# Channel mixer over nine groups of 512 tokens in place of sixteen pieces of 320 and 256

## The chip, the cores and the metric

The kernel runs on one core of a Trainium2 chip. The metric is device time in microseconds (us), from the first to the last instruction, lower is better. TensorE (PE) multiplies, VectorE (DVE) and ScalarE (ACT) work on vectors, GpSimd (POOL) does elementwise work beside them, and the queue of SyncE (SP) issues all DMAs of this kernel. Each engine takes its instructions in a fixed order and waits on semaphores for the others.

## The reference

Eight batches of 576 tokens, eight heads of 64 channels. Heads 0 to 3 attend to a query's last 32 positions, heads 4 to 7 to earlier positions of the same residue modulo 32. The result, 512 channels a token, goes through a token mixer (576 to 256 to 576 positions) and a channel mixer (512 to 1536 to 512 channels), each with its residual:

```python
mask_local = (rel >= 0) & (rel < stride)
mask_strided = (rel >= 0) & (pos[None, :] % stride == pos[:, None] % stride)
...
attn_out = softmax(where(mask, q @ k.T / sqrt(64), -1e9)) @ v
x = attn_out.transpose(0, 2, 1, 3).reshape(B, S, H * D)
h = relu(x.transpose(0, 2, 1) @ w_tok1) @ w_tok2
u = x + h.transpose(0, 2, 1)
return u + relu(u @ w_ch1) @ w_ch2
```

The mixers' weights come as float64. The kernel cuts every operand of a mixer into a high and a low fp32r part and adds three products (high by high, high by low, low by high).

## The kernel before

**Local heads** (`local_unit`) are done in units of three chunks of 128 tokens and two heads, six units for a pair of batches: loads lq, lk, lv (L125 to L127), scores on PE (L133), softmax on DVE and ACT, transposes, products with v, and xl written to DRAM.

**Strided heads** are done in two ways. Those of batches 0 and 1 are on PE (`strided_pe`: scores L221, exponentials, transposes, products, then ex on DVE, L249, which goes to DRAM as xs, L259); their operands eq, ek, ev come by `strided_load`. Those of batches 2 to 7 are on GpSimd and VectorE (`strided`): after loads of sa and sb (L266, L267), 18 products of rising width, 64 to 1152 elements (L275, POOL), each followed by a reduce into ss (L276, DVE), a softmax, the load of v into sa, again 18 products (L290) and reduces into sb (L291), and four DMAs to xs. This text calls that work of one batch a pass, its halves the QK half and the AV half, and the passes of batches 2 to 7 in a row the lane. The tiles sa and sb have one buffer each, so a pass loads its operands after the one before has done with them.

**The token mixer** loads a batch's x (L299, L301), cuts it into xh (ACT, L313) and xlo (DVE, L314), multiplies by w_tok1 (`tok1`, L323, 56 matmuls of 256 columns a batch), cuts the hidden values into hh and hl, and in `tok2` transposes x (L341) and adds the products with w_tok2 (L346); the result is cut into uh (ACT, L349) and ul (DVE, L350).

**The channel mixer** (`mlp`) works on a piece, the 320 or the 256 tokens that one batch has in `PIECES`. For each of 12 chunks of the hidden size, `up_proj` does 12 matmuls into h (L439), cut into gh (ACT, L442) and gl (DVE, L443), and `down_proj` 12 matmuls into the four accumulators acc (L451): 288 matmuls a piece, 16 pieces. Midway, POOL adds uh and ul into ot (L464); at the end DVE adds acc to ot (L468) and DMAs bring the columns to out_t (L471 to L474).

**Order of the work.** The program is built as one long list, and a scheduler with a simulated timeline sets a fixed order on each engine from it. Other work is put into the list between the steps of a piece by the tables `ins0` and `ins1`: `tok2` of the same batch's second piece, late local units of the next pair, `do_load`, `do_tok1` and `do_tok2` of the next batch, and `do_strided(b + 2)`, which lists a pass two batches ahead at a lower priority. During piece 0 the last weights are loaded and cut (`do_pieces`; w_raw, L83) and batch 1's strided heads go between on PE; `second_ends` closes their pool and lists the first pass, batch 2's, at the second step of piece 1.

## Time and profile before

| what | value |
|---|---|
| median of 3 runs | 912.22 us (911.15 to 917.72) |
| span of the profiled execution | 912.1 us |
| mean granted TensorE clock in it | 0.979 |
| TensorE busy | 871.2 us, 96% of the span |
| VectorE busy | 514.4 us, 56% |
| GpSimd busy | 408.9 us, 45% |
| ScalarE busy | 261.5 us, 29% |

The profiled execution's span is 0.1 us from the median, so sums are made against 912.1. Rows of the profile give an engine, a line (L439 is line 439 of the kernel), an operation and the tiles as output<-inputs; xN is a count. In rows in order of time the first two numbers are the start and the length in us, and what stands in square brackets is idle time ahead of the instruction and what ended it. Matmuls are pipelined: a matmul's length is longer than the distance to the next one, and it is the distance that costs.

### The profile page before, as it was taken

The page shows a single profiled execution, that of the slowest core. Times are in us where ns is not written, and L with a number is a line of the kernel's source. Part 1 is how long each engine was busy: PE and PEld are TensorE (multiplying, and loading weights), DVE is VectorE, ACT ScalarE, POOL GpSimd, SP SyncE. Part 2 cuts the span into 40 slices and gives each one's busy share as a digit, 9 for nine tenths or more (in the row PEclk, how much of TensorE's full clock was granted, in tenths as well). Part 3 has the DMA queues.
Part 4 walks back from the last instruction along what each step waited for, and adds up shares of the span by engine and source line. Part 5 has one row for each costly group of instructions (what it writes and reads, how often), then busy time and mean ns, then how long its engine had stood idle before and what let it go on. Part 6 is the DMA issues. An engine that isn't in the chain of part 4 may idle for free.

```text
span 912.1 us, 20133 instructions
## 1 busy us (share of the span) xinstructions
PE 871.2 (96%) x8176; PEld 823.4 (90%) x8176; DVE 514.4 (56%) x1308; ACT 261.5 (29%) x840; POOL 408.9 (45%) x322
## 2 busy tenths in 40 slices
PE   6798999999989799999998999999999999999998
PEld 4667989899989599999998899898999999999998
DVE  2978794787478647757767864787232231222121
ACT  4755563222222123222231222322232221121111
POOL 0324342789397567959657594967001010101010
PEclk9968999999999699999999999999999999999999
DMA  8566644030642133230362024211131020100010
GB/s 249 174 212 192 198 152 132 28 95 23 175 137 80 55 105 89 75 105 24 95 175 57 27 81 129 88 53 50 47 108 32 1 81 1 30 1 24 1 31 24
DMA packets 71289, 78.36 MB, mean 86 GB/s; under 512 B 24100, under 2 KB 60068, under 8 KB 71196
## 3 DMA queue, kind: packets, MB, share of 16 engines
q1 hardware_dynamic: 71196, 77.07, 28.5%
q8 instruction: 64, 1.05, 0.5%
q14 instruction: 29, 0.24, 0.1%
HBM read 58.63 MB, written 18.28 MB: 84 GB/s over the span
## 4 chain that ended last, share of the span: by engine, by line
PE 64%; DVE 13%; DMA 9%; POOL 8%; SPq 2%; ACT 2%; issue 2%; DVEq 0%; POOLq 0%; ACTq 0%
PE h L439 24%; PE acc L451 23%; PE t L346 6%; POOL sprod L275 6%; PE t L323 5%; DVE xlo L314 5%; PE t L341 2%; POOL sprod L290 2%; DMA sb<-in_ks 2%; DVE ss L276 2%; DVE sb L291 1%; DMA x<-xs 1%; DVE w_f L89 1%; DVE w_f L88 1%; DMA w_raw<-in_wt 1%
## 5 line engine op out<-in xcount | busy, mean ns | idle before, releaser
L439 PE MATMUL h<-uh,w1h 128*128 128x320 f32 (+1 forms) x768 | 227.6, 300 | 3.9 <-DVE gl L443 3.2
L439 PE MATMUL h<-uh,w1l 128*128 128x320 f32 (+1 forms) x768 | 229.0, 299 | 0.0
L439 PE MATMUL h<-ul,w1h 128*128 128x320 f32 (+1 forms) x768 | 228.6, 299 | 0.0
L451 PE MATMUL acc<-gl,w2h 128*128 128x320 f32 (+1 forms) x768 | 227.3, 299 | 0.0
L451 PE MATMUL acc<-gh,w2l 128*128 128x320 f32 (+1 forms) x768 | 223.9, 299 | 0.0
L451 PE MATMUL acc<-gh,w2h 128*128 128x320 f32 (+1 forms) x768 | 220.1, 300 | 2.3 <-ACT gh L442 1.6
L275 POOL TENSOR_TENSOR sprod<-sb,sa 128x64 f32<-128x64 f32 (+8 forms) x108 | 160.2, 1517 | 63.0 <-DMA sb<-in_ks 47.6
L443 DVE SCALAR_TENSOR_TENSOR gl<-h,gh 128x320 fp32r<-128x320 f32 (+1 forms) x192 | 86.2, 452 | 163.4 <-ACT gh L442 163.2
L290 POOL TENSOR_TENSOR sprod<-sa,ss 128x64 f32<-128x64 f32 (+8 forms) x108 | 154.9, 1468 | 47.2 <-DVE ss L285 23.0
L464 POOL TENSOR_TENSOR ot<-uh,ul 128x320 f32<-128x320 f32 (+1 forms) x64 | 52.5, 836 | 262.5 <-DMA out_t<-ot 251.2
L442 ACT ACTIVATE gh<-h 128x320 fp32r<-128x320 f32 (+1 forms) x192 | 78.0, 409 | 309.9 <-PE h L439 309.4
L439 PEld LDWEIGHTS h<-uh,w1h 128*128 128x128 f32 x768 | 145.8, 191 | 5.6 <-DVE gl L443 4.0
L439 PEld LDWEIGHTS h<-uh,w1l 128*128 128x128 f32 x768 | 146.3, 191 | 0.6
L439 PEld LDWEIGHTS h<-ul,w1h 128*128 128x128 f32 x768 | 146.4, 191 | 0.3
L451 PEld LDWEIGHTS acc<-gl,w2h 128*128 128x128 f32 x768 | 146.0, 190 | 0.7 <-DVE gl L443 0.2
L451 PEld LDWEIGHTS acc<-gh,w2h 128*128 128x128 f32 x768 | 142.1, 190 | 4.5 <-ACT gh L442 1.8
L451 PEld LDWEIGHTS acc<-gh,w2l 128*128 128x128 f32 x768 | 144.8, 190 | 0.9
L276 DVE TENSOR_REDUCE ss<-sprod 128x1 f32<-128x64 f32 (+8 forms) x108 | 83.8, 780 | 43.1 <-POOL sprod L275 42.7
L291 DVE TENSOR_REDUCE sb<-sprod 128x64 f32<-128x64 f32 (+8 forms) x108 | 83.8, 780 | 26.6 <-POOL sprod L290 25.9
L314 DVE TENSOR_TENSOR xlo<-x,xh 128x256 fp32r<-128x256 f32 x80 | 66.9, 852 | 49.3 <-ACT xh L313 49.2
L323 PE MATMUL t<-xlo,t1h 128*128 128x256 f32 (+1 forms) x160 | 51.7, 333 | 13.5 <-DVE xlo L314 13.4
L313 ACT CAST xh<-x 128x256 fp32r<-128x256 f32 x80 | 32.1, 406 | 107.6 <-PE t L323 65.2
(79 smaller groups left out, 1080.7 us busy)
## 6 DMA issues: line engine op xcount, KB each, us to landing
w_raw<-in_w SPq DMA_DIRECT2D x24, 512.0 KB
out_t<-ot SPq DMA_DIRECT2D x64, 128.0 KB
lv<-in_vw SPq DMA_DIRECT2D x20, 384.0 KB
lk<-in_kT SPq DMA_DIRECT2D x20, 208.0 KB
x<-xs SPq DMA_DIRECT2D x8, 512.0 KB
lq<-in_qT SPq DMA_DIRECT2D x20, 192.0 KB
x<-xl SPq DMA_DIRECT2D x7, 512.0 KB
sa<-in_qs SPq DMA_DIRECT2D x6, 576.0 KB
```

What stands on the lines that cost most here:

```text
L275: nc.gpsimd.tensor_tensor(out=pr, in0=k_t[:, :n, :], in1=q_t[:, i:i + 1, :].to_broadcast([P, n, D]), op=ALU.mult)
L276: nc.vector.tensor_reduce(out=s_t[:, i, :n], in_=pr, axis=AX.X, op=ALU.add)
L290: nc.gpsimd.tensor_tensor(out=pr, in0=v_t[:, :, :n], in1=s_t[:, i:i + 1, :n].to_broadcast([P, D, n]), op=ALU.mult)
L291: nc.vector.tensor_reduce(out=o_t[:, i], in_=pr, axis=AX.X, op=ALU.add)
L314: nc.vector.tensor_tensor(out=xlo, in0=x, in1=xh.bitcast(F32), op=ALU.subtract)
L323: nc.tensor.matmul(ph[m][:, o:o + DT], l, r, start=(c == 0 and k == 0 and o == 0), stop=(short and k == 1 and o + DT == n), skip_group_che ...
L346: nc.tensor.matmul(pu[:, :n], l[:, cs], r[:, m, s0:s0 + n], start=False, stop=(m == 1 and k == 2), skip_group_check=True)
L439: nc.tensor.matmul(ph[:, :n], l[:, cc, fs], r, start=(cc == 0 and k == 0), stop=(cc == NCC - 1 and k == 2))
L442: nc.scalar.activation(out=gh[:, :n], in_=ph[:, :n], func=AF.Relu)
L443: nc.vector.scalar_tensor_tensor(out=gl[:, :n], in0=ph[:, :n], scalar=0.0, in1=gh[:, :n].bitcast(F32), op0=ALU.max, op1=ALU.subtract)
L451: nc.tensor.matmul(acc[cc][:, :n], l[:, fc, cs], r[:, :n], start=(fc == 0 and k == 0), stop=(fc == NFC - 1 and k == 2))
L464: nc.gpsimd.tensor_tensor(out=o_t[:, :n], in0=uh.bitcast(F32), in1=ul.bitcast(F32), op=ALU.add)
```

## The change

The 4608 tokens are taken as one row, cut into nine groups of 512. Group 0 is the first 512 tokens of batch 0; group g has the last 64·g tokens of batch g−1 and the first 512 − 64·g of batch g; group 8 is the end of batch 7. `tok2` of a batch therefore comes in two parts of other widths for each batch, from 64 to 512 columns: the head of batch g+1 during group g, the tail of batch g during group g itself. With that:

- every matmul of the channel mixer moves 512 columns; there are 9 × 288 in place of 16 × 288, and `tok1` moves 512 columns in 28 matmuls in place of 256 in 56;
- the tables of inserts have 24 half-steps, before and after each `down_proj`; `do_strided(g + 2)` is listed at half-step 12 of group g, the first pass (batch 2's) at the end of group 0, the late local units at other places;
- the residual comes at the end of a group: DVE adds acc and uh, POOL adds ul (DVE in the last group), and one DMA takes the 128 × 512 tile, 36 in all; ot has three buffers in place of four;
- batch 1's eq, ek and ev have one buffer in place of two; the weight w_tok2 is loaded in its own order of columns.

The diff, without comments and cut to its core:

```diff
+GT = 512
+NG = B * S // GT
...
-        q_t = pool.tile([P, S], F32, name="eq")
-        k_t = pool.tile([P, S], F32, name="ek")
-        v_t = pool.tile([RP, NRG, 2, D], F32, name="ev")
+        q_t = pool.tile([P, S], F32, name="eq", bufs=1 if b else 2)
+        k_t = pool.tile([P, S], F32, name="ek", bufs=1 if b else 2)
+        v_t = pool.tile([RP, NRG, 2, D], F32, name="ev", bufs=1 if b else 2)
...
-            for o in range(0, n, DT):
-                x = x_t[:, c, cs.start + o:cs.start + o + DT]
-                xh = pool.tile([P, DT], F32R, name="xh")
-                xlo = pool.tile([P, DT], F32R, name="xlo")
-                nc.scalar.copy(out=xh, in_=x)
-                nc.vector.tensor_tensor(out=xlo, in0=x, in1=xh.bitcast(F32), op=ALU.subtract)
...
+            x = x_t[:, c, cs]
+            xh = pool.tile([P, DM], F32R, name="xh")[:, :n]
+            xlo = pool.tile([P, DM], F32R, name="xlo")[:, :n]
+            nc.scalar.copy(out=xh, in_=x)
+            nc.vector.tensor_tensor(out=xlo, in0=x, in1=xh.bitcast(F32), op=ALU.subtract)
...
+                for k, (l, r) in enumerate(terms):
+                    nc.tensor.matmul(ph[m], l, r, start=(c == 0 and k == 0), stop=(short and k == 1))
...
+    def new_u(pool):
+        return [[pool.tile([P, GT], F32R, name=f"u{k}", bufs=NCC) for k in "hl"] for _ in range(NCC)]
+    def tok2(ps_t, x_t, h, us, b, tail, ccs):
+        t0, t1 = (GT - 64 * b, S) if tail else (0, GT - 64 * b)
+        n, g0 = t1 - t0, 0 if tail else 64 * b
         for cc in ccs:
             cs = slice(P * cc, P * cc + P)
             pu = ps_t.tile([P, 512], F32, name="t")
-            for i, c in enumerate(PIECES[piece]):
-                w = min(P, S - P * c)
-                nc.tensor.matmul(pu[:, P * i:P * i + w], x_t[:w, c, cs], ident[:w, :w],
-                                 is_transpose=True, start=(i == 0), stop=False, skip_group_check=True)
+            t = t0
+            while t < t1:
+                c, r = divmod(t, P)
+                w = min(P - r, t1 - t, S - t)
+                if c == NSC - 1 and t0 % P:
+                    r = 64
+                nc.tensor.matmul(pu[:, t - t0:t - t0 + w], x_t[r:r + w, c, cs], ident[r:r + w, r:r + w],
+                                 is_transpose=True, start=(t == t0), stop=False, skip_group_check=True)
+                t += w
             for m in range(2):
                 hh, hl = h[m]
                 for k, (l, r) in enumerate(((hh, t2h), (hh, t2l), (hl, t2h))):
-                    nc.tensor.matmul(pu[:, :n], l[:, cs], r[:, m, s0:s0 + n], start=False, stop=(m == 1 and k == 2), skip_group_check=True)
-            uh = pool.tile([P, n], F32R, name=f"uh{piece}", bufs=NCC)
-            ul = pool.tile([P, n], F32R, name=f"ul{piece}", bufs=NCC)
+                    nc.tensor.matmul(pu[:, :n], l[:, cs], r[:, m, t0:t1], start=False, stop=(m == 1 and k == 2), skip_group_check=True)
+            uh, ul = (u[:, g0:g0 + n] for u in us[cc])
...
-    def mlp(b, piece, us, inserts):
-        n = PLEN[piece]
-        acc = [ps_acc.tile([P, 512], F32, name=f"acc{cc}") for cc in range(NCC)]
+    def mlp(grp, us, inserts):
+        acc = [ps_acc.tile([P, GT], F32, name=f"acc{cc}") for cc in range(NCC)]
...
-        res = []
         for fc in range(NFC):
             if fc + 2 < NFC:
                 up_proj(fc + 2)
-            for f in inserts.get(fc, ()):
+            for f in inserts.get(2 * fc, ()):
                 f()
-            if fc == NFC // 2:
-                for uh, ul in us:
-                    o_t = up.tile([P, PLEN[0]], F32, name="ot", bufs=NCC)
-                    nc.gpsimd.tensor_tensor(out=o_t[:, :n], in0=uh.bitcast(F32), in1=ul.bitcast(F32), op=ALU.add)
-                    res.append(o_t)
             down_proj(fc)
-        for cc, o_t in enumerate(res):
-            nc.vector.tensor_tensor(out=o_t[:, :n], in0=acc[cc][:, :n], in1=o_t[:, :n], op=ALU.add)
-            ro = outT[P * cc:P * cc + P, S * b:S * b + S]
-            if piece == 0:
-                nc.sync.dma_start(out=ro[:, :256], in_=o_t[:, :256])
-                nc.sync.dma_start(out=ro[:, 512:], in_=o_t[:, 256:n])
-            else:
-                nc.sync.dma_start(out=ro[:, 256:512], in_=o_t[:, :n])
+            for f in inserts.get(2 * fc + 1, ()):
+                f()
+        for cc, (uh, ul) in enumerate(us):
+            o_t = up.tile([P, GT], F32, name="ot", bufs=3)
+            nc.vector.tensor_tensor(out=o_t, in0=acc[cc], in1=uh.bitcast(F32), op=ALU.add)
+            add = nc.vector if grp == NG - 1 else nc.gpsimd
+            add.tensor_tensor(out=o_t, in0=o_t, in1=ul.bitcast(F32), op=ALU.add)
+            nc.sync.dma_start(out=outT[P * cc:P * cc + P, GT * grp:GT * grp + GT], in_=o_t)
...
-    def do_tok2(b, piece):
-        state[piece] = tok2(up if piece else up0, ps_t, state["x"], state["h"], piece, range(NCC))
+    def do_tok2(b, tail):
+        g = b + tail
+        if g not in us:
+            us[g] = new_u(up if g % 2 else xp)
+        tok2(ps_t, state["x"], state["h"], us[g], b, tail, range(NCC))
...
-        at(ins0, 1 if b else 0, lambda: do_tok2(b, 1))
-        if b == 0:
+                at(i0 + k, go)
+        if g < B:
+            at(2, lambda: do_tok2(g, True))
+        if g == 0:
             pools["second"] = tc.tile_pool(name="second", bufs=2, reuse_waits="tile")
             second = pools["second"].__enter__()
-            for fc in range(NFC):
-                at(ins0, fc, lambda: do_pieces(2))
+            for i in range(2 * NFC):
+                at(i, lambda: do_pieces(1))
             lane = strided_lanes(second, 1)
             for i in range(13):
-                for g in lane:
-                    at(ins0, min(i, NFC - 1), step(g))
-            at(ins0, NFC - 1, staging_ends)
-            at(ins1, 1, second_ends)
-        elif b + 2 < B:
-            at(ins1, 0, lambda: do_strided(b + 2))
-        if not last:
-            p = b // 2 + 1
-            if p < B // 2:
-                if b == 0:
-                    late_unit(ins1, 8, p, 0)
-                elif b == 1:
-                    for i in range(1, 6):
-                        late_unit(ins0, 2 * i - 2, p, i)
-                elif b % 2 == 0:
-                    for i in range(2):
-                        late_unit(ins0, 3 + 4 * i, p, i)
-                    late_unit(ins1, 0, p, 2)
-                else:
-                    for i in range(3, 6):
-                        late_unit(ins0, 2 + 3 * (i - 3), p, i)
-            at(ins1, 1, lambda: do_load(b + 1))
-            at(ins1, 4 if b == 0 else 2 if b % 2 else 5, lambda: do_tok1(b + 1))
-            at(ins1, 9, lambda: do_tok2(b + 1, 0))
-        mlp(b, 0, state[0], ins0)
-        mlp(b, 1, state[1], ins1)
+                for f in lane:
+                    at(i, step(f))
+            at(2 * NFC - 1, staging_ends)
+            at(2 * NFC - 1, second_ends)
+        elif g + 2 < B:
+            at(12, lambda: do_strided(g + 2))
+        if g == 1:
+            for i in range(6):
+                late_unit(3 * i, 1, i)
+        elif g < B - 2 and g:
+            p = g // 2 + 1
+            if g % 2 == 0:
+                for i in range(2):
+                    late_unit(6 + 8 * i, p, i)
+            else:
+                for i in range(2, 4):
+                    late_unit(4 * i - 8, p, i)
+                for i in range(4, 6):
+                    late_unit(4 * i - 4, p, i)
+        if g + 1 < B:
+            at(13, lambda: do_load(g + 1))
+            at(16, lambda: do_tok1(g + 1))
+            at(20, lambda: do_tok2(g + 1, False))
+        mlp(g, us.pop(g), ins)
```

In the changed kernel the lines are a few off: up_proj's matmuls are L441, down_proj's L453, gl L445, the lane's reduces L275 and L290, its products L274 and L289, ul L355, xlo L312, the two adds of ot L467 and L469, ex L248.

Two places show what moved. The first is on VectorE where the first channel-mixer stretch ends and the lane begins. In the kernel before, batch 1's last ex tiles stand among the first piece's adds, and four gl of the second piece stand ahead of the lane's first reduce:

```order
L249 TENSOR_TENSOR ex3_1851<-t_1949,em_1890 126x3x64
L468 TENSOR_TENSOR ot_1753<-acc0_1206,ot_1753 128x320
L468 TENSOR_TENSOR ot_1755<-acc1_1207,ot_1755 128x320
L468 TENSOR_TENSOR ot_1757<-acc2_1208,ot_1757 128x320
L249 TENSOR_TENSOR ex2_1856<-t_1957,em_1904 126x64
```

In the changed kernel group 0's adds come first, and after them the softmax (es, em) and the ex tiles of batch 1's last step, then the next batch's xlo and the lane's first reduce:

```order
L467 TENSOR_TENSOR ot_2224<-acc2_1205,uh_750 128x512
L223 ISA es_1687,em_1688<-t_1686,mask2_sb_66 126x126
...
L467 TENSOR_TENSOR ot_2228<-acc3_1206,uh_752 128x512
...
L248 TENSOR_TENSOR ex3_1657<-t_1770,em_1688 126x3x64
L248 TENSOR_TENSOR ex2_1662<-t_1778,em_1702 126x64
...
L312 TENSOR_TENSOR xlo_1910<-x_1832,xh_1909 128x512
L312 TENSOR_TENSOR xlo_1920<-x_1832,xh_1919 128x512
L275 TENSOR_REDUCE ss_2090<-sprod_2094 128x1
```

So the last strided step on PE now stands behind all of group 0, and the lane's first pass behind it.

The second place is on VectorE at the start of batch 5's channel mixer in the kernel before; these are the last rows of the lane, the reduces of sprod_9165, _9168 and _9171 being the 16th to 18th of batch 7's AV half, beside the last piece of batch 4 (ot) and the ul of batch 5:

```order
L291 TENSOR_REDUCE sb_9119<-sprod_9165 128x64
L350 TENSOR_TENSOR ul0_8223<-t_8212,uh0_8222 128x320
L468 TENSOR_TENSOR ot_8117<-acc0_7556,ot_8117 128x256
L291 TENSOR_REDUCE sb_9119<-sprod_9168 128x64
L350 TENSOR_TENSOR ul0_8237<-t_8226,uh0_8236 128x320
...
L291 TENSOR_REDUCE sb_9119<-sprod_9171 128x64
L350 TENSOR_TENSOR ul0_8251<-t_8240,uh0_8250 128x320
L350 TENSOR_TENSOR ul0_8265<-t_8254,uh0_8264 128x320
L350 TENSOR_TENSOR ul1_8406<-t_8396,uh1_8405 128x256
L443 SCALAR_TENSOR_TENSOR gl_8330<-h_8316,gh_8329 128x320
```

The same stretch in the changed kernel, where the ul are those of batch 5's head in group 5 and gl_6098 is that group's first; sprod_6646 to _6661 are the 10th to 15th of the AV half of the same pass:

```order
L290 TENSOR_REDUCE sb_6618<-sprod_6646 128x64
...
L355 TENSOR_TENSOR ul_5334<-t_5996,uh_5333 128x192
L290 TENSOR_REDUCE sb_6618<-sprod_6649 128x64
L355 TENSOR_TENSOR ul_5336<-t_6007,uh_5335 128x192
L290 TENSOR_REDUCE sb_6618<-sprod_6652 128x64
L355 TENSOR_TENSOR ul_5338<-t_6018,uh_5337 128x192
L290 TENSOR_REDUCE sb_6618<-sprod_6655 128x64
L290 TENSOR_REDUCE sb_6618<-sprod_6658 128x64
L355 TENSOR_TENSOR ul_5340<-t_6029,uh_5339 128x192
L290 TENSOR_REDUCE sb_6618<-sprod_6661 128x64
L445 SCALAR_TENSOR_TENSOR gl_6098<-h_6084,gh_6097 128x512
```

The channel mixer's sixth unit of work, which was batch 5 and is now group 5, stands at almost the same place of the lane; before it lie five batches (2880 tokens) in the one kernel and five groups (2560 tokens) in the other.

More of the change, by code (lines that the diff above doesn't have):

```diff
@@ L116, in load_t2 @@
         for c, w in enumerate(rows):
-            load_split(stage, t2h[:, c, :DM], t2l[:, c, :DM], w[:, :256], w[:, 512:], w[:, 256:448])
-        load_split(stage, t2h[:, :, DM:], t2l[:, :, DM:], *(w[:, 448:512] for w in rows))
+            load_split(stage, t2h[:, c, :DM], t2l[:, c, :DM], w[:, :DM])
+        load_split(stage, t2h[:, :, DM:], t2l[:, :, DM:], *(w[:, DM:] for w in rows))
     def local_unit(pool, ps_t, p, hp, c0, n, into=None):
@@ L308, in tok1 @@
             short = c == NSC - 1
-            for o in range(0, n, DT):
-                x = x_t[:, c, cs.start + o:cs.start + o + DT]
-                xh = pool.tile([P, DT], F32R, name="xh")
-                xlo = pool.tile([P, DT], F32R, name="xlo")
-                nc.scalar.copy(out=xh, in_=x)
-                nc.vector.tensor_tensor(out=xlo, in0=x, in1=xh.bitcast(F32), op=ALU.subtract)
-                for m in range(2):
-                    ms = slice(P * m, P * m + P)
-                    if short:
-                        terms = ((t1h[:64, c, ms], xlo[:64]), (t1l[:, c, ms], xh))
-                    else:
-                        terms = ((t1h[:, c, ms], xh), (t1h[:, c, ms], xlo), (t1l[:, c, ms], xh))
-                    for k, (l, r) in enumerate(terms):
-                        nc.tensor.matmul(ph[m][:, o:o + DT], l, r, start=(c == 0 and k == 0 and o == 0),
-                                         stop=(short and k == 1 and o + DT == n), skip_group_check=True)
+            x = x_t[:, c, cs]
[3 more added lines that the diff above has]
+            nc.vector.tensor_tensor(out=xlo, in0=x, in1=xh.bitcast(F32), op=ALU.subtract)
+            for m in range(2):
+                ms = slice(P * m, P * m + P)
+                if short:
+                    terms = ((t1h[:64, c, ms], xlo[:64]), (t1l[:, c, ms], xh))
+                else:
+                    terms = ((t1h[:, c, ms], xh), (t1h[:, c, ms], xlo), (t1l[:, c, ms], xh))
+                for k, (l, r) in enumerate(terms):
+                    nc.tensor.matmul(ph[m], l, r, start=(c == 0 and k == 0), stop=(short and k == 1))
         for m in range(2):
@@ L438, in up_proj @@
                 for k, (l, r) in enumerate(((w1h, uh), (w1h, ul), (w1l, uh))):
[L439 to L443 removed]
+                    nc.tensor.matmul(ph, l[:, cc, fs], r, start=(cc == 0 and k == 0), stop=(cc == NCC - 1 and k == 2))
+            gh = up.tile([P, GT], F32R, name="gh")
+            gl = up.tile([P, GT], F32R, name="gl")
+            nc.scalar.activation(out=gh, in_=ph, func=AF.Relu)
+            nc.vector.scalar_tensor_tensor(out=gl, in0=ph, scalar=0.0, in1=gh.bitcast(F32), op0=ALU.max, op1=ALU.subtract)
             g[fc] = (gh, gl)
@@ L450, in down_proj @@
                 for k, (l, r) in enumerate(((w2h, gh), (w2h, gl), (w2l, gh))):
-                    nc.tensor.matmul(acc[cc][:, :n], l[:, fc, cs], r[:, :n], start=(fc == 0 and k == 0), stop=(fc == NFC - 1 and k == 2))
+                    nc.tensor.matmul(acc[cc], l[:, fc, cs], r, start=(fc == 0 and k == 0), stop=(fc == NFC - 1 and k == 2))
         up_proj(0)
         up_proj(1)
-        res = []
         for fc in range(NFC):
@@ L518, in staging_ends, with at, late_unit @@
         pools["late"] = ctx.enter_context(tc.tile_pool(name="late", bufs=1, side="right", reuse_waits="tile"))
-    for b in range(B):
-        last = b == B - 1
-        ins0, ins1 = {}, {}
-        def at(d, fc, f):
-            d.setdefault(fc, []).append(f)
-        def late_unit(d, fc, p, i):
+    for g in range(NG):
+        ins = {}
+        def at(i, f):
+            ins.setdefault(i, []).append(f)
+        def late_unit(i0, p, i):
             gen = []
```

26 lines of the change are left out of this document (6 added, 20 removed).

## The prediction

> **What bounds the kernel now.** I began with the busy times and went on to the chain of waits in order of time:
>
> ```profile
> span 912.1 us, 20133 instructions
> PE 871.2 (96%) x8176; PEld 823.4 (90%) x8176; DVE 514.4 (56%) x1308; ACT 261.5 (29%) x840; POOL 408.9 (45%) x322
> ...
> 156.19 5.63 DMA sb<-in_ks
> 242.63 10.71 POOL sprod L275 x11
> 561.54 4.14 DMA sb<-in_ks
> 565.80 12.59 POOL sprod L275 x12
> 868.33 5.28 PE acc L451 x36
> 873.61 2.88 PE h L439 x24
> ```
>
> TensorE is busy 96% of the span, and the end of the chain is nothing but its matmuls: 36 of 320 columns in 5.28 us are 146.7 ns each, 24 of 256 columns in 2.88 us are 120.0 ns. The 64 columns between cost 26.7 ns, so a matmul takes 13.3 ns and a column 0.417 ns. But earlier in the same chain stand the products of the strided lane and the loads ahead of them. So I looked at the lane by itself, its first and its last pass, and at the matmul that follows it:
>
> ```profile
> L275 POOL TENSOR_TENSOR sprod<-sb,sa x18: 324/1526/2689, 162.0 to 190.5; 128x64 f32<-128x64 f32 x1, 128x128 f32<-128x128 f32 x1, 128x192 f32<-128x192 f32 x1, 128x256 f32<-128x256 f32 x1
> ...
> 556.61 0.49 SPq L293
> ...
> L275 POOL TENSOR_TENSOR sprod<-sb,sa x18: 322/1503/2697, 565.8 to 592.1; 128x64 f32<-128x64 f32 x1, 128x128 f32<-128x128 f32 x1, 128x192 f32<-128x192 f32 x1, 128x256 f32<-128x256 f32 x1
> ...
> L290 POOL TENSOR_TENSOR sprod<-sa,ss x18: 323/1538/2532, 600.1 to 627.4; 128x64 f32<-128x64 f32 x1, 128x128 f32<-128x128 f32 x1, 128x192 f32<-128x192 f32 x1, 128x256 f32<-128x256 f32 x1
> ...
> 615.37 4.07 POOL L290 TENSOR_TENSOR sprod<-sa,ss 128x832 f32<-128x832 f32 x2 [1.16 <-DVE sb L291]
> 620.73 4.43 POOL L290 TENSOR_TENSOR sprod<-sa,ss 128x960 f32<-128x960 f32 x2 [1.29 <-DVE sb L291]
> ...
> 628.95 0.46 PE L439 MATMUL h<-uh,w1h 128*128 128x320 f32 x2
> ```
>
> The lane starts at 162.0. Its six passes begin (565.8 − 162.0)/5 = 80.8 us apart. The last one goes from 565.8 to 627.4 plus a last product of 2.5, 64 us, and from one pass's first output DMA (556.61) to the next one's first product (565.8) are 9.2 us. With some 2 us between the last product and that DMA a pass that nothing holds up takes about 75 us. Batch 5's channel mixer begins at 628.95, just as the lane ends; from there to 912.1, 283.1 us, everything is TensorE's. Up to there the two are nearly in balance.
>
> That they can hold each other up is seen once, between batches 1 and 2:
>
> ```profile
> 297.41 1.07 DVE L291 TENSOR_REDUCE sb<-sprod 128x64 f32<-128x896 f32 x1
> ...
> 299.06 2.56 DVE L314 TENSOR_TENSOR xlo<-x,xh 128x256 fp32r<-128x256 f32 x2
> ...
> 301.34 0.58 PE L323 MATMUL t<-xlo,t1h 128*128 128x256 f32 x1 [3.50 <-DVE xlo L314]
> ...
> 311.33 0.47 PE L346 MATMUL t<-t2l,hh 128*128 128x320 f32 x1
> 311.60 0.47 PE L346 MATMUL t<-t2h,hl 128*128 128x320 f32 x1
> ...
> 300.00:350.00 50.00, 46.67 (x316) 42.53 (x317) 29.09 (x57) 11.69 (x35) 29.90 (x24) 0.83 0.26 74
> ```
>
> xlo stands in VectorE's fixed order behind a reduce of the lane; TensorE waits 3.5 us for it, and then its 320-column matmuls come 0.27 us apart in place of 0.147, in a stretch with a granted clock of 0.83. The Trainium skill, "TensorE: Matmul & The Clock Gate", "HAM oscillation", says that idle gaps above about 3.4 us halve the clock; the trace agrees, with those 0.27 us. So a wait for the lane costs more than its own length.
>
> **The matmuls.** The channel mixer's issue time is now 8 × 288 × (0.1467 + 0.120) = 614.4 us. A 512-column matmul by the line above is 13.3 + 512 × 0.417 = 226.7 ns; 9 × 288 of them are 587.5, a gain of 26.9 us (65.3 us a group). Its bound from above is two of 256, 240 ns, at which nothing is gained (622); from below pure columns, 213 ns, −62. I take the line, since both its points are of these very matmuls. The Trainium skill, same page, "Back-to-back issue gap", gives columns/2.4 plus 2.5 ns, 215.8 for 512; but it would give 135.8 and 109.2 for 320 and 256, where the trace has 146.7 and 120.0. By it the stretch after the lane, below, would be 12.6 us shorter. `tok1`: 56 × 0.120 = 6.7 us becomes 28 × 0.2267 = 6.3, 3 us in all.
>
> `tok2`'s parts of 64, 128 and 192 columns (six of 16, 24 matmuls each) are of widths the trace doesn't have. By the line they cost 40, 67 and 93 ns. The nearest narrow ones are the scores of batch 1:
>
> ```profile
> 135.68 0.92 PE L221 MATMUL t<-ek,eq 64*126 64x126 f32 x6
> 136.53 0.42 PE L451 MATMUL acc<-gh,w2h 128*128 128x320 f32 x1
> ```
>
> Six of 126 columns in 0.85 us are 142 ns, 1.13 ns a column; so the upper prices are 72, 144 and 217, and all six parts cost between nothing and 2 × 24 × (32 + 77 + 124) = 11 us more. I take 2, since the line is from the same type of operand. After the lane only the heads of batches 6 and 7 are such: 0 to 2.6.
>
> **The residual.**
>
> ```profile
> L464 POOL TENSOR_TENSOR ot<-uh,ul 128x320 f32<-128x320 f32 (+1 forms) x64 | 52.5, 836 | 262.5 <-DMA out_t<-ot 251.2
> ...
> L468 DVE TENSOR_TENSOR ot<-acc,ot 128x320 f32<-128x320 f32 x32 | 14.1, 479 | 7.6 <-PE acc L451 7.6
> L468 DVE TENSOR_TENSOR ot<-acc,ot 128x256 f32<-128x256 f32 x32 | 11.9, 413 | 4.9 <-PE acc L451 4.9
> ...
> 908.22 0.41 DVE ot L468
> ```
>
> GpSimd's adds are the same sum of columns, 5.9 us a group (836 ns × 512/288 × 4), hidden in its idle time (45% busy) except that four of them stand among the lane's products and now wait for a group's end. Behind these products wait the lane's reduces, and behind those, on VectorE, the next group's ul and gl. At the end of the kernel two adds of about 0.7 us (413 ns and 1.03 ns a column) replace the one of 0.41: +1, and with the wider last DMA I take +2. Fewer DMAs for out_t free nothing that anyone waits for.
>
> **The lane's start.** It is what moves most. Of group 0's neighbours:
>
> ```profile
> 131.09 0.33 SPq L83 DMA_DIRECT2D w_raw<-in_w  x1
> 142.01 0.33 SPq L125 DMA_DIRECT2D lq<-in_qT  x1
> ...
> L439 PE MATMUL h<-uh,w1h x60: 280/309/634, 66.7 to 148.2; 128*128 128x320 f32 x48, 128*128 128x256 f32 x12
> ...
> L451 PE MATMUL acc<-gh,w2h x48: 305/309/418, 85.9 to 144.5; 128*128 128x320 f32 x48
> ...
> L249 DVE TENSOR_TENSOR ex<-t,em x8: 210/282/357, 111.7 to 147.2; 126x192 f32<-126x192 f32 x4, 126x64 f32<-126x64 f32 x4
> ```
>
> Piece 0 goes from 66.7 to about 146 (its last matmuls follow the 144.5 of the row), 80 us, of which 288 × 0.1467 = 42 are its own and 38 are other work and waits for weights (the last w_raw is issued at 131.09, and the units that need the staging's room at 142.01). Group 0 has 65.3 of its own and the same other work: it ends at 66.7 + 65.3 + 38 = 170, or at 159 if 11 us of waiting now lie under the longer matmuls; I take 165. The order then has, behind its adds, batch 1's last strided step, because that batch's second pair of heads, single-buffered, is loaded only after the last weights and after the units' lq. Eight ex in 35.5 us are 4.4 each; two remain, 9 us. From the last ex (147.2) to the lane's first product (162.0) were 14.8: xs out, x in, sa and sb. The sum is 165 + 9 + 15 = 189; I take 188 (178 to 196), 26 later than now.
>
> **What hangs on the lane.** In the order of VectorE, batch 5's head in group 5 and that group's first gl stand behind the 14th and 15th AV reduces of the last pass; batch 5 now stands behind the last. Groups 1 to 4 stand at the same places of passes 2 to 6 as batches 1 to 4 did. A group of 512 tokens thus has the same share of the lane as 576 before, and at that point 2560 tokens are done, not 2880. TensorE doesn't need that long: 8 pieces and the rest of the program took it 628.95 − 193 (the start of batch 1's stretch) = 436, four groups 46 less, so it waits.
>
> The point lies five periods and 55 us (565.8 to 620.7, where products 13 and 14 are done) after the lane's start. For the period I take 77, nearer to the unhindered 75 than to 80.8, since the lane is now what others wait for. To that 7 us, a guess between 0 and the 19 that the stall after 296 cost (piece 3 ends at 296.3, piece 4 starts at 315.3): six late units, x of batch 2 and four adds now meet between groups 1 and 2. So group 5 begins at 188 + 385 + 55 + 7 = 635.
>
> **After it**, four groups: 4 × 65.3 = 261. The six pieces now after 629 are 3 × 288 × 0.2667 = 230.4 of 283.1, which leaves 52.7 for the last two token mixers, local units and the end. These stay, with −1 for `tok1`, +1 for the 64 columns more of batch 5's tail, +2 for the end and +4 for narrow parts and the gap at the start of group 6: 320. The sum is 635 + 320 = **955 us**.
>
> **The rivals.**
>
> *TensorE sets the time (faster).* Waits for the lane would be absorbed by h's and u's buffers. Then 912.1 − 26.9 − 3 + 2 (narrow) + 2 (end) + 2 (more transposes) = 888. For it speaks the 96% of TensorE and that the first stall (296 to 315) is the only large one now. Group 5 would have to begin at 568, so the lane's period be (568 − 188 − 55)/5 = 65, or 67 from a start at 178; even for under 903 it must be below 70. The products alone take 27 + 30 us, the reload 11: 68. Chance 0.08.
>
> *No change.* The lane starts at 178 and its period is 72, as GpSimd has fewer interruptions: 178 + 360 + 55 + 320 = 913. Chance 0.11.
>
> *The lane is slower.* It keeps 80.8 and loses 19 at group 1: 188 + 404 + 55 + 19 + 320 = 986. This needs reduces that wait behind gl in VectorE's order, as they do now; waits then halve the clock and feed on each other. Chance 0.16 for 970 and above.
>
> *Wide matmuls gain nothing.* At 240 ns the stretch after the lane is 15 longer: 970; both rows speak against it, 0.03. The same page of the Trainium skill also states a sustained 131 ns for 512 columns: the 1152 matmuls after the lane would be 110 shorter, 845; since 256 columns already take 120.0 here, 0.01.
>
> The rest, 0.61, is the forecast, 921 to 970.
>
> **Numbers.** A difference of 1% is about what a measurement of this kernel can tell. Below 903 are the first rival and the last one, 0.09; within 903 to 921 lies no change, 0.11; above it 0.80. The range goes from 908, which takes in the early start with the short period, to 988, the slow lane's own value; about 0.09 is left below and 0.07 above.
>
> **What would show it.** Right: the lane's first product near 188 and batch 1's last ex behind group 0's last matmul; group 5's first up_proj near 635, after the 14th AV reduce of the last pass; TensorE's idle time before ul, gl or xlo in 190 to 635, with the granted clock below 1 in those stretches; 512-column matmuls 0.227 apart; 320 us after the lane. Wrong: a lane that starts before 175 or a period under 70, or groups 1 to 4 back to back at full clock, which would bring the time to 890.

## The result, and the profile after

The changed kernel takes 965.14 us (median of 4 runs, 963.07 to 968.13) where the kernel before takes 911.68 on the same chip: a ratio of 1.0565, 95% interval 1.0518 to 1.0612. The forecast was 955, range 908 to 988. So the number lies in the range, and most of the terms came out; the reason behind it did not, as the experiments show.

Busy times and two rows of the 40 slices, from the page of the changed kernel:

```profile
span 966.4 us, 15148 instructions
...
PE 880.4 (91%) x5980; PEld 695.0 (72%) x5980; DVE 493.3 (51%) x1165; ACT 242.3 (25%) x721; POOL 399.4 (41%) x290
...
PE   6887999499974899989996999899989999999997
...
PEclk9987999799995899989997999799997999999999
```

TensorE is now idle 86 us (966.4 − 880.4; 41 before), and the granted clock dips again and again. The dips lie between the groups. The same kernel's busy times, cut at each group's last down_proj and the next one's first up_proj; columns are PE, PEld, DVE, ACT and POOL busy, then the granted clock, the DMA share and GB/s:

```profile
169.70:200.90 31.20, 18.26 (x64) 12.82 (x64) 13.80 (x29) 6.59 (x18) 16.49 (x15) 0.73 0.30 97
200.90:282.10 81.20, 81.20 (x647) 64.28 (x652) 49.97 (x114) 17.75 (x59) 57.46 (x40) 1.00 0.26 73
282.10:329.80 47.70, 23.91 (x344) 16.85 (x345) 35.94 (x84) 12.89 (x48) 32.37 (x23) 0.64 0.37 116
329.80:411.70 81.90, 81.88 (x513) 66.40 (x511) 55.99 (x102) 18.11 (x51) 60.87 (x43) 1.00 0.25 71
411.70:422.50 10.80, 8.12 (x70) 5.83 (x71) 5.40 (x12) 1.62 (x3) 7.37 (x9) 0.76 0.87 256
...
508.00:529.90 21.90, 13.03 (x132) 8.77 (x131) 17.92 (x34) 4.76 (x17) 20.42 (x11) 0.69 0.29 95
...
612.30:624.80 12.50, 7.99 (x70) 5.59 (x69) 8.58 (x14) 1.51 (x3) 12.50 (x10) 0.62 0.40 132
...
714.40:728.50 14.10, 11.10 (x130) 7.61 (x128) 6.14 (x23) 4.66 (x17) 1.67 (x1) 0.74 0.17 56
```

Inside groups 1 to 6 TensorE is busy from end to end, at a clock of 0.96 to 1.00. Between groups 0 to 6 there are six stretches without a channel-mixer matmul, 138 us in sum, at a clock of 0.62 to 0.76. The kernel before has one such stretch, between its fourth piece and its fifth:

```profile
296.30:315.30 19.00, 13.15 (x45) 9.65 (x44) 13.26 (x16) 3.12 (x7) 10.66 (x7) 0.59 0.18 60
```

What TensorE does in the longest one of the changed kernel, after group 1, in order of time:

```profile
282.02 0.73 PE L132 MATMUL t<-lk,lq 64*32 64x64 f32 x48
287.69 0.48 PE L152 MATMUL t<-ident,ls 128*128 128x128 f32 x1 [4.95 <-ACT ls L144]
...
297.00 1.13 PE L132 MATMUL t<-lk,lq 64*32 64x64 f32 x48 [5.98 <-DVE lx L171]
...
308.11 1.11 PE L132 MATMUL t<-lk,lq 64*32 64x64 f32 x48 [4.94 <-DMA lk<-in_kT]
...
310.27 0.63 PE L320 MATMUL t<-xlo,t1h 128*128 128x512 f32 x1
310.69 0.63 PE L320 MATMUL t<-xh,t1l 128*128 128x512 f32 x1
```

Three local units, tok1 and the first half of tok2 stand there one behind the other, each step waiting for the one before on ScalarE, VectorE or a DMA, with nothing for TensorE to do meanwhile. The waits of 5 us cost twice: behind the last of them, at 310.27, matmuls of 512 columns come 0.42 us apart in place of 0.227.

Priced at the spacing that the same forms have inside the groups (the lower quartile of each form), the matmuls of all these stretches are 45 us of 140 (with 1.8 after group 6); 95 are idle time and half clock. In the kernel before that is 13 of 19. This difference, +82, less the 27 us of issue that the wide matmuls save, gives 55, and 54 were measured (966.4 − 912.1). The small terms cancel: the transposes of x and the end cost some 8 us more, the start and the waits inside pieces some 8 less (distances from one matmul's start to the next, in both traces).

Of the terms that were computed from rows, most came out. The lane and two places of TensorE in the changed kernel:

```profile
L274 POOL TENSOR_TENSOR sprod<-sb,sa x108: 321/1552/2692, 186.7 to 599.5; 128x64 f32<-128x64 f32 x6, 128x128 f32<-128x128 f32 x6, 128x192 f32<-128x192 f32 x6, 128x256 f32<-128x256 f32 x6
...
L274 POOL TENSOR_TENSOR sprod<-sb,sa x18: 325/1502/2675, 574.4 to 599.5; 128x64 f32<-128x64 f32 x1, 128x128 f32<-128x128 f32 x1, 128x192 f32<-128x192 f32 x1, 128x256 f32<-128x256 f32 x1
...
624.77 0.68 PE L441 MATMUL h<-uh,w1h 128*128 128x512 f32 x1
...
935.24 2.72 PE acc L453 x12
```

The lane starts at 186.7 (188 was forecast), its period is (574.4 − 186.7)/5 = 77.5 us (77), group 5 begins at 624.8 (635 was forecast, 10 later), and twelve matmuls of 512 columns take 2.72 us, 226.7 ns each (226.7). From group 5 to the end are 341.6 us, where 320 were forecast.

### The profile page after: what moved, and what is told of

Read it like the earlier page. It is cut to its first block, busy times and chain, and to the rows that moved or that the text cites. A ratio compares the mean times of both kernels' runs of the same rounds, so it can differ in the third digit from the quotient of the medians.

```text
span 966.4 us, 15148 instructions
## 1 busy us (share of the span) xinstructions
PE 880.4 (91%) x5980; PEld 695.0 (72%) x5980; DVE 493.3 (51%) x1165; ACT 242.3 (25%) x721; POOL 399.4 (41%) x290
## 4 chain that ended last, share of the span: by engine, by line
PE 46%; POOL 16%; DVE 13%; DMA 10%; issue 10%; ACT 3%; SPq 2%; POOLq 0%; DVEq 0%; ACTq 0%
PE h L441 19%; PE acc L453 15%; POOL sprod L274 7%; POOL sprod L289 7%; PE t L352 6%; PE t L346 3%; DMA sb<-in_ks 2%; DVE w_f L88 2%; DVE w_f L89 2%; DMA x<-xs 2%; DVE xlo L312 1%; PE t L320 1%; DVE lz L147 1%; DVE ss L275 1%; DVE w_f L87 1%
## 5 line engine op out<-in xcount | busy, mean ns | idle before, releaser
L274 POOL TENSOR_TENSOR sprod<-sb,sa 128x64 f32<-128x64 f32 (+8 forms) x108 | 159.9, 1516 | 70.9 <-DMA sb<-in_ks 60.4
L289 POOL TENSOR_TENSOR sprod<-sa,ss 128x64 f32<-128x64 f32 (+8 forms) x108 | 155.4, 1477 | 51.7 <-DVE ss L284 29.1
L441 PE MATMUL h<-ul,w1h 128*128 128x512 f32 x432 | 172.4, 399 | 0.0
L441 PE MATMUL h<-uh,w1l 128*128 128x512 f32 x432 | 171.3, 396 | 0.0
L445 DVE SCALAR_TENSOR_TENSOR gl<-h,gh 128x512 fp32r<-128x512 f32 x108 | 73.9, 687 | 188.6 <-ACT gh L444 188.1
L441 PE MATMUL h<-uh,w1h 128*128 128x512 f32 x432 | 169.1, 403 | 1.0 <-DVE gl L445 1.0
L453 PE MATMUL acc<-gh,w2l 128*128 128x512 f32 x432 | 169.0, 391 | 0.0
L453 PE MATMUL acc<-gl,w2h 128*128 128x512 f32 x432 | 168.9, 391 | 0.0
L453 PE MATMUL acc<-gh,w2h 128*128 128x512 f32 x432 | 164.2, 392 | 1.0 <-ACT gh L444 1.0
L469 POOL TENSOR_TENSOR ot<-ot,ul 128x512 f32<-128x512 f32 x32 | 41.1, 1302 | 278.8 <-DVE ot L467 274.6
L275 DVE TENSOR_REDUCE ss<-sprod 128x1 f32<-128x64 f32 (+8 forms) x108 | 84.3, 782 | 49.9 <-POOL sprod L274 49.8
L290 DVE TENSOR_REDUCE sb<-sprod 128x64 f32<-128x64 f32 (+8 forms) x108 | 84.2, 782 | 32.4 <-POOL sprod L289 31.5
L441 PEld LDWEIGHTS h<-uh,w1h 128*128 128x128 f32 x432 | 82.1, 192 | 18.6 <-DVE gl L445 1.5
L441 PEld LDWEIGHTS h<-ul,w1h 128*128 128x128 f32 x432 | 82.1, 190 | 17.3 <-DVE ul L355 0.4
L441 PEld LDWEIGHTS h<-uh,w1l 128*128 128x128 f32 x432 | 82.0, 190 | 16.5
L453 PEld LDWEIGHTS acc<-gh,w2h 128*128 128x128 f32 x432 | 80.7, 188 | 18.3 <-ACT gh L444 1.4
L453 PEld LDWEIGHTS acc<-gl,w2h 128*128 128x128 f32 x432 | 81.1, 188 | 16.9
L453 PEld LDWEIGHTS acc<-gh,w2l 128*128 128x128 f32 x432 | 81.1, 188 | 16.9
L355 DVE TENSOR_TENSOR ul<-t,uh 128x512 fp32r<-128x512 f32 (+7 forms) x64 | 29.1, 455 | 58.6 <-ACT uh L354 58.6
L312 DVE TENSOR_TENSOR xlo<-x,xh 128x512 fp32r<-128x512 f32 (+1 forms) x45 | 42.0, 945 | 32.8 <-ACT xh L311 32.6
```

What stands on the lines that cost most here:

```text
L274: nc.gpsimd.tensor_tensor(out=pr, in0=k_t[:, :n, :], in1=q_t[:, i:i + 1, :].to_broadcast([P, n, D]), op=ALU.mult)
L275: nc.vector.tensor_reduce(out=s_t[:, i, :n], in_=pr, axis=AX.X, op=ALU.add)
L289: nc.gpsimd.tensor_tensor(out=pr, in0=v_t[:, :, :n], in1=s_t[:, i:i + 1, :n].to_broadcast([P, D, n]), op=ALU.mult)
L290: nc.vector.tensor_reduce(out=o_t[:, i], in_=pr, axis=AX.X, op=ALU.add)
L312: nc.vector.tensor_tensor(out=xlo, in0=x, in1=xh.bitcast(F32), op=ALU.subtract)
L441: nc.tensor.matmul(ph, l[:, cc, fs], r, start=(cc == 0 and k == 0), stop=(cc == NCC - 1 and k == 2))
```

## The experiments

Two theories stood against each other. **L**, the prediction's: the lane on GpSimd and VectorE sets the pace of groups 1 to 5 through VectorE's fixed order. **P**: the lists put token mixer and local units behind a group's last matmul on TensorE, where nothing covers their waits, whatever the lane does. A ratio is to the kernel before, measured on the same chip, with its 95% interval.

**The lane's work left out, in both kernels.** In `strided`, only the first of the 18 products and reduces of each half stays:

```diff
         for i in range(NJ):
             n = i + 1
             pr = pool.tile([P, NJ * D], F32, name="sprod", bufs=2)...
+            if i: continue
             nc.gpsimd.tensor_tensor(out=pr, ...)
             nc.vector.tensor_reduce(...)
```

The changed kernel so:

> The changed kernel with 17 of the 18 products and 17 of the 18 reduces left out in each half of a lane pass (outputs of the strided heads of batches 2 to 7 are mostly zeros); loads, softmax and output DMAs stay. Theory L (the lane sets the pace of groups 1 to 5): groups follow each other as fast as TensorE can, some 885 to 905 us. Theory P (the order on TensorE puts token mixer and local units behind a group's last matmul, where nothing covers their waits; in the changed kernel's trace the stretches between groups 0 to 6 sum to 138 us): the order behind each group is the same here, 6 of 7 stretches stay, though without queueing behind the lane's reduces; 925 to 950 us, with stretches between groups of 90 us or more in sum.

And the kernel before:

> The kernel before with the same work left out. Both theories: the stall after piece 3 (19 us) goes, and little else, since TensorE is at 96%: 885 to 900 us. The distance to the run without the lane of the changed kernel says what the change does with the lane out of the way: L: the changed one is 5 us slower to 20 us faster; P: it is 30 to 60 slower.

They took 941.72 and 889.30 us, in one execution each. Busy times of the changed kernel without the lane's work, four of its six stretches, and the one stretch of the kernel before without it:

```profile
PE 875.1 (93%) x5980; PEld 694.3 (74%) x5980; DVE 314.8 (33%) x961; ACT 243.7 (26%) x721; POOL 96.0 (10%) x92
...
171.60:199.80 28.20, 16.69 (x63) 11.88 (x63) 10.37 (x26) 6.95 (x19) 5.14 (x7) 0.76 0.55 170
282.40:320.40 38.00, 22.59 (x296) 16.61 (x297) 10.85 (x47) 11.85 (x45) 2.90 (x3) 0.64 0.46 132
...
496.50:511.50 15.00, 11.13 (x132) 8.12 (x131) 6.55 (x23) 4.76 (x17) 2.86 (x2) 0.77 0.36 109
593.90:601.90 8.00, 7.13 (x69) 5.04 (x69) 3.11 (x7) 1.51 (x3) 3.25 (x3) 0.68 0.52 173
```

```profile
291.50:300.00 8.50, 7.71 (x27) 5.68 (x28) 2.62 (x6) 1.62 (x3) 0.87 (x1) 0.70 0.10 34
```

GpSimd falls from 399 to 96 us of work, and the stretches stay, 112 us in sum. The lane is worth some 23 us in the changed kernel and 20 in the kernel before; the distance between the two is 52.4 without it and 53.5 with it. L falls: of the change's cost hardly anything comes by the lane, though the lane costs each kernel its 20 us. The stretch of the kernel before was expected to go; 8.5 of its 19 us stay.

The account by stretches closes less well here. Beyond their matmuls the stretches hold 72 us in the changed kernel and 5 in the kernel before; this difference less 27 is 40 of the 52. The start, the transposes of x and the end add some 11 there, and nothing offsets them. So that the account above closes to 1 us is partly luck.

**The token mixer listed earlier**, from group 2 on:

```diff
-            at(13, lambda: do_load(g + 1))
-            at(16, lambda: do_tok1(g + 1))
-            at(20, lambda: do_tok2(g + 1, False))
+            at(8 if g > 1 else 13, lambda: do_load(g + 1))
+            at(11 if g > 1 else 16, lambda: do_tok1(g + 1))
+            at(16 if g > 1 else 20, lambda: do_tok2(g + 1, False))
```

> The changed kernel, where from group 2 on the load of x, tok1 and tok2's head are listed at half-steps 8, 11 and 16 of a group in place of 13, 16 and 20; all work stays. In TensorE's order less stands behind groups 2 to 6 (behind group 2 and 4 the 28 rows of tok1 and most of tok2 are gone); behind group 1 all stays. L: group 5 stands at the 9th AV reduce of the last pass in place of the 15th, so 0 to 10 us faster than the changed kernel, 955 to 966. P: the stretches after groups 2 and 4 (10.8 and 12.5 us) nearly close and those after 3, 5 and 6 shrink: 925 to 945.

950.42 us, ratio 1.0431 (1.0389 to 1.0473): 12 to 15 us less than the changed kernel (by the ratios and by the medians), between the two expectations. Its stretches after groups 3 and 5; the one between them, after group 4 (607.6 to 608.6), is 1.0 us long:

```profile
502.60:517.60 15.00, 8.59 (x120) 6.49 (x121) 11.76 (x29) 4.25 (x16) 15.00 (x10) 0.66 0.40 128
...
698.00:709.30 11.30, 7.76 (x119) 5.57 (x118) 4.17 (x21) 4.03 (x16) 3.80 (x4) 0.66 0.59 182
```

The stretches after groups 2, 4 and 6 close, as P said; those after 3 and 5 shrink by a third at most (15.0 for 21.9, 11.3 for 14.1), and some of the gain goes into longer groups, where the same work now stands (group 6: 91.7 us, 85.0 before). The lane's last product ends at 637, 642 in the changed kernel: it hardly takes notice.

**The local units listed elsewhere too** (three in each group, a pair's sixth in the group after, the token mixer in a group's first half):

```diff
+    UNITS = {1: [(0, 1, 0), (2, 1, 1), (4, 1, 2), (6, 1, 3), (17, 1, 4)], 2: [(0, 1, 5), (14, 2, 0), (18, 2, 1)], ...}
+    TIMES = {0: (13, 16, 20), None: (3, 6, 11), 1: (10, 13, 18), 3: (6, 9, 14), 5: (6, 9, 14)}
```

> As the run before, and local units are listed elsewhere too: the sixth unit of a pair in the group after, three units a group, the token mixer in the first half of a group. Behind groups 2, 6 and 7 nothing is left, behind 4 only tok2's end, behind 1 two units in place of three. L: the lane starts at 187 as before and its pace stays 77: 945 to 966. P: 25 to 50 faster than the changed kernel: 915 to 940.

964.27 us: no gain at all, a miss for P's number and a hit for L's. Two of its stretches, after groups 3 and 5:

```profile
493.80:523.80 30.00, 15.30 (x92) 10.84 (x93) 19.96 (x29) 4.57 (x8) 27.60 (x20) 0.69 0.24 77
703.20:722.20 19.00, 11.87 (x44) 8.80 (x43) 5.73 (x10) 4.46 (x8) 4.19 (x4) 0.77 0.30 97
```

After groups 2 and 6 nothing is left, but after 3 and 5 there is more than in the run before it (30.0 and 19.0 against 15.0 and 11.3), and some groups are longer (group 6: 93.3 us). So places in a list alone didn't do. The side work of an odd group, local units that must be written to DRAM and loaded again before tok1 and tok2 can follow, is one chain; that it is about as long as a group, so that what is pulled out of one stretch comes back in the next, is a reading of this and wasn't measured. The lane has a small part in it: the last unit's lx begins at 496.9, behind the lane's fourth reduce and three of the group's adds, 2.5 us after the products that it needs.

**The grouping alone undone**: all other edits stay, the sixteen pieces and their tables come back.

```diff
-NG = B * S // GT
+GROUPS = [(S * b + o, n) for b in range(B) for o, n in ((0, 320), (320, 256))]
+NG = len(GROUPS)
```

> The changed kernel with the grouping alone undone: sixteen pieces (320 and 256 tokens, in order) with the inserts of the kernel before; tok1's 512 columns, the residual at the end, three ot, batch 1's single buffers and w_tok2's order stay. In TensorE's order only one piece (the fourth, as in the kernel before) has work behind it. P (uncovered stretches between groups): 903 to 918 us, as the kernel before. If one of the edits that stay cost the 54 us, up to 965. L (lane): its start is then no later than some 170, so 905 to 925.

913.22 us, ratio 1.0000 (0.9977 to 1.0023), as both theories would have it. tok1's wide matmuls, the residual at the end with its ring of three, batch 1's single buffers and w_tok2's order together cost and bring nothing beyond 2 us. The whole loss is in the groups and their lists.

**The converse: stretches made in the kernel before**, by later places in its own list.

```diff
-            at(ins1, 1, lambda: do_load(b + 1))
-            at(ins1, 4 if b == 0 else 2 if b % 2 else 5, lambda: do_tok1(b + 1))
-            at(ins1, 9, lambda: do_tok2(b + 1, 0))
+            at(ins1, 6, lambda: do_load(b + 1))
+            at(ins1, 9, lambda: do_tok1(b + 1))
+            at(ins1, 11, lambda: do_tok2(b + 1, 0))
```

> The kernel before, with the load of x, tok1 and tok2's first piece listed later in a batch's second piece (steps 6, 9 and 11 in place of 1, 2 to 5 and 9); nothing else is changed. In TensorE's order most of tok1 and a part of tok2 now stand behind seven pieces (before: one). P: each such stretch costs some 7 to 15 us beyond its matmuls, as in the changed kernel's trace: six new ones, 950 to 1000 us. L: the lane's place is hardly moved and its pace stays: 905 to 920.

952.01 us, ratio 1.0405 (1.0362 to 1.0447), as P said. Three of its seven stretches:

```profile
181.90:210.30 28.40, 19.40 (x114) 14.87 (x113) 22.43 (x34) 4.89 (x11) 14.40 (x12) 0.60 0.20 61
...
651.80:663.90 12.10, 11.06 (x52) 8.67 (x51) 4.01 (x9) 3.25 (x7) 0.86 (x1) 0.77 0.13 43
...
857.80:867.90 10.10, 9.07 (x39) 7.00 (x39) 3.17 (x7) 2.43 (x5) 0.86 (x1) 0.77 0.16 52
```

Clocks of 0.60 to 0.80 and lengths of 10 to 28 us, with the pieces of 320 and 256 untouched. The lane's last product ends at 643.7 here (629.9 in the kernel before), and batch 5's channel mixer begins at 663.9, 20 us behind it: TensorE sets this time, and the stretches come also after the lane. With this P stands from both sides: the stretches can be made without the groups, and the kernel without the groups has but one, of 9.3 us.

**Groups where there is cover.** Ten pieces for batches 0 to 4, then 512, 512, 512 and 192 tokens:

```diff
+FB = 5
+GROUPS = [(S * b + o, n) for b in range(FB) for o, n in ((0, 320), (320, 256))]
+GROUPS += [(t, min(GT, B * S - t)) for t in range(S * FB, B * S, GT)]
```

> As the run before for batches 0 to 4 (ten pieces), then groups of 512, 512, 512 and 192 tokens over batches 5 to 7, with local units, token mixer and tok2 listed in a group's first two thirds; nothing stands behind those groups in TensorE's order. Fourteen stretches of matmuls in place of sixteen. P: two times 288 x 13.3 ns = 7.7 us are gained and nothing is lost: 895 to 908, 5 to 9 under the run before. If 512 columns cost twice 256 (240 ns), 11 us more than that, so no gain.

910.32 us, ratio 0.9972 (0.9945 to 0.9998); 2.9 under the sixteen pieces by the medians, less than the 5 to 9 expected, and above the range of 895 to 908. From batch 5's first matmul to the end, the sixteen pieces first, then this kernel:

```profile
625.10:913.40 288.30, 281.92 (x2263) 269.17 (x2262) 72.53 (x188) 52.72 (x145) 23.69 (x27) 0.99 0.11 34
```

```profile
625.80:907.50 281.70, 275.97 (x1675) 230.33 (x1673) 67.02 (x157) 48.03 (x121) 21.45 (x18) 0.99 0.11 35
```

There the two profiled executions have 6.6 of the 7.7 us. But executions of one kernel differ by more than that (905.8 to 916.7 for this one), and 2.9 us are near the noise of the medians. So the gain that the line gives isn't shown for the whole time; what is shown is that groups with nothing behind them cost nothing.

**Batches 0 and 1 as pieces, groups from batch 2 on**:

```diff
+FB = 2
```

> Batches 0 and 1 as four pieces with the inserts of the kernel before (one local unit, needed only by batch 3, goes to the first group), batches 2 to 7 as groups of 512 (six, and one of 384), with the token mixer listed in a group's first half: eleven pieces. Against the run that listed the token mixer early, this takes away the stretches behind groups 0 and 1 (31.6 and 50.0 us there, 20 and 38 beyond the matmuls in them). In TensorE's order work stands behind two groups (a unit's end, tok1 and tok2) and a little behind a third. P: 950 less some 55, more 8 to 14 for two pieces more and the stretches: 900 to 920 us. L (the lane, whose start is some 25 us earlier, at 160): 950 less 20 to 25, 925 to 935.

919.97 us, ratio 1.0086 (1.0058 to 1.0114): at the end of P's range and below L's. Against the run with the early token mixer 30 us are gone with the stretches behind groups 0 and 1. Two stretches are left, 32.4 and 23.7 us. In the first, TensorE's wait and, from the chain of waits, what it waited for:

```profile
477.80 0.74 POOL sprod L277
478.64 0.05 DVEq L174
478.93 0.64 DVE lx L174 x2
479.58 0.45 SPq L199
...
483.34 4.25 DMA x<-xl
487.62 0.63 ACT xh L314
```

```profile
488.29 1.22 PE L323 MATMUL t<-xh,t1h 128*128 128x512 f32 x2 [13.79 <-ACT xh L314]
```

A local unit's result, its six writes to DRAM, the load of x, the cast: the chain of an odd group, uncovered. But ahead of it stands the lane: lx is placed in VectorE's order behind the lane's fourth reduce, whose product starts at 477.80, and begins at 478.93, though TensorE's last products for it ended at 474.5. So up to 4.4 of the 13.8 us are a wait of the kind that L named (three of the group's own adds, of 0.68 us each, stand in between). Such waits are there; by the two kernels without the lane's work they aren't what the change costs.

**One local unit moved**, in the kernel with ten pieces and four groups:

```diff
-                    for i in range(1, 6):
+                    for i in range(1, 5):
                         late_unit(4 * i - 4, 1, i)
...
+                    if b == 2:
+                        late_unit(2, 1, 5)
```

> The run with ten pieces and four groups over batches 5 to 7, where one local unit (of batches 2 and 3, needed by batch 3 only) goes from batch 1 to the first piece of batch 2. Nothing stands behind any piece now; the run before it had 9 us behind the fourth. P: 6 to 12 us under the run before it, 898 to 905, below the kernel before by about 1%. L: that stall came from reduces of the lane ahead of xlo, which stay: 907 to 911.

907.49 us, ratio 0.9958 (0.9932 to 0.9984), 1 to 3 us under the kernel with ten pieces and four groups (by the ratios and by the medians), not 6 to 12. The number lies in L's range, but the stall, which L said would stay, is gone: nothing is left of the 9.4 us behind the fourth piece. Beyond its matmuls that stretch held some 5.5 (by the spacings inside pieces), and that is what there was to win. It is the fastest version here that does all the work, 0.4% below the kernel before. In none of these versions do groups of 512 run through batches 0 to 4 without stretches; that this can be had isn't shown.

**The last four groups made even**, 448, 448, 448 and 384:

```diff
-GROUPS += [(t, min(GT, B * S - t)) for t in range(S * FB, B * S, GT)]
+GROUPS += [(S * FB + 448 * i, min(448, B * S - S * FB - 448 * i)) for i in range(4)]
```

> The run before it (907.5 us) with the last four groups of 448, 448, 448 and 384 tokens in place of 512, 512, 512 and 192. In the changed kernel's trace the matmuls of 64, 128 and 192 columns all come 109 to 112 ns apart, and the last group of 192 took 32.3 us for its 288 (26.9 by the line of 13.3 ns and 0.417 ns a column). If that floor is what took most of the 7.7 us which two stretches less should give, four groups all wider than 256 give it back: some 5 us less, 901 to 904, 0.8 to 1.1% under the kernel before. If the floor has nothing to do with it: 907.

908.97 us, ratio 0.9969 (0.9945 to 0.9993): not faster than the run before it. By the groups' first and last matmuls its last four take 276.4 us, as before (276.0). The two traces tell where the 5 us went, by the distances from one matmul's start to the next in these stretches: the channel-mixer matmuls are only 3.0 shorter (228.4 for 231.5), since those of 448 columns come 202 to 206 ns apart where the line has 200; and the transposes of x (L350), more of which are now of 64 columns, take 10.5 in place of 7.0.

## Why the prediction was right, and where it was wrong

**The matmuls**: right. 226.7 ns for 512 columns, to the digit. The formula of the Trainium skill, "TensorE: Matmul & The Clock Gate", "Back-to-back issue gap" (215.8), is not borne out, as for the narrower ones. For the narrowest part of tok2 the bounds failed: 64 columns were to cost 40 to 72 ns and cost 112 (last section). It is small here, 24 matmuls a part.

**The residual**: the run with sixteen pieces, which has it at the end with its ring of three, shows no cost beyond 2 us, together with the other edits that it keeps.

**The lane's start**: right, 186.7 for 188, by the steps named: group 0's last matmul at 169.7 (159 to 170), the last strided step behind it, then the loads. Its period, 77.5 for 77, too.

**What hangs on the lane**: here is the step that failed. It read the order of VectorE, where each group stands at the same place of the lane as a batch did, as "so it waits". A shared place in one engine's order says that the two go together, not which one holds the other. The sentence that TensorE "doesn't need that long" priced its work as if all of it were covered, 436 less 46 for four groups. Measured, groups 1 to 4 with the stretches behind them took 424 us (200.9 to 624.8), 12 less than batches 1 to 4. With the lane's work left out they took 402 (199.8 to 601.9), and batches 1 to 4 took 418 (186.8 to 604.4), 16 less. So the stretches ate 30 to 34 of the 46 us, with the lane or without it, and the lane adds some 20 to either kernel. That the sum came within 11 us is luck: it put group 5 at 635, which began 10 us sooner, and 320 us behind it, where there were 22 more, and it gave to the lane the time that the stretches took.

**After it**: 341.6 for 320. The mis-sized term is the 52.7 of token mixers and units, which "stay", with +4 for gaps: outside the groups stood 14.1 + 1.8 us and groups 5 to 7 were longer than their matmuls. It is the same error as above, small enough here to be seen as a term.

**The rivals**: "TensorE sets the time" named the true cause, with a wrong price. It gave 2 us each to narrow parts, transposes and the end, and nothing to stretches between groups, so 888. The order of TensorE would have told: 28 matmuls of tok1, 144 score matmuls of three units and 12 products of tok2 stand between group 1's last down_proj and group 2's first up_proj, where in the kernel before only one of 16 pieces has such work. The one stretch of that kind in the trace (19 us, where the changed kernel has six) was read as a stall by the lane; without the lane's work 8.5 of them stay. It was the price that the forecast lacked: 13 us beyond its matmuls, and in the changed kernel some 16 for each of six.

**What would show it right**: idle time of TensorE before xlo and the like from 190 to 635, with a low clock, was there, and none of the forecast's signs of being wrong came: its signs could not tell the two causes apart. What TensorE waited for, in us in total, times and longest, in the changed kernel and then without the lane's work (where the lines of the token mixer are 3 further down):

```profile
PE t L320 <- DVE xlo L312: 12.8, 12, 3.6
PE t L320 <- ACT xh L311: 11.8, 3, 10.7
PE t L132 <- DMA lk<-in_kT: 11.2, 3, 4.9
```

```profile
PE t L323 <- ACT xh L314: 11.7, 2, 10.4
PE t L132 <- DMA lk<-in_kT: 11.2, 3, 4.9
...
PE t L323 <- DVE xlo L315: 2.8, 6, 0.9
```

xlo, which stands between the lane's reduces, was the mark that the forecast named, and most of it is the lane's; the waits for xh and lk, which follow the loads of x and of a unit's keys, are as long without the lane. Those were the mark of the other cause.

## What to carry to other kernels

When larger tiles shorten the main loop, the cover for what is threaded through it gets shorter too: here a group's 65 us of matmuls had to cover what a batch's 77 us covered before. Before counting the saving, list what stands between the last matmul of one tile and the first of the next on the busy engine, and price that as a bare chain of latencies. A place in a fixed order shared by two engines' work proves no direction; leaving one side's work out does. And a hit of the number doesn't prove the reason.
